# Longer loads in the planner's books, the softmax sums' column left in PSUM, and three slots of the arena given to weights earlier

## The chip, the cores and the metric

One Trainium2 chip; the program runs on one of its cores. The metric is device time in microseconds of one execution, lower is better. Three runs of the kernel before gave 725.32, 720.64 and 724.05 us (median 724.05).

## The reference, cut to what matters

Three stages follow each other, all in float32: rotary attention over B = 4 batches of H = 8 heads (S = 576 tokens, D = 64), a soft mixture of 8 experts with 4 slots each, and a two-layer MLP.

```python
q_rot, k_rot = rotate(q), rotate(k)                      # (4, 8, 576, 64)
scores = q_rot @ k_rot.T / sqrt(64)
attn = exp(scores - max); attn = attn / (attn.sum(-1) + 1e-09)
x = (attn @ v)                                           # 2304 tokens x 512
logits = x @ phi                                         # 512 x 32 slots
slot_input = softmax(logits, over tokens).T @ x          # 8 experts x 4 slots x 512
slot_out[e] = relu(slot_input[e] @ w1[e]) @ w2[e]        # 512 -> 1024 -> 512
x = softmax(logits, over slots) @ slot_out
out = square(relu(x @ w_in)) @ w_out                     # 512 -> 2048 -> 512
```

## The kernel before, in words

**Attention.** Two heads make a *pair* (`NP` = 16 pairs), one head in each half of the 128 partitions. For a pair the kernel:

- loads k, q and their half-swapped copies into one of two buffers `raws[p % 2]` (four slices of 128 x 576; `load`, L296, three DMAs `SEGS` of 64 partitions each, 1152 KB together);
- applies the rotation with six tensor-tensor operations, three for each of k and q (`rope_pair`, L313, recorded at L309, `arena<-arena` in the trace), on VectorE or GpSimd, whichever the planner picks;
- splits each rotated tensor into a rounded half on ScalarE (`parts_pair`, L337, tile `tE`, three buffers `his`) and a remainder on VectorE or GpSimd (L309 again, `tL<-arena,tE`). When both remainders exist, `raws[p % 2]` is free and the load of pair p + 2 can be issued;
- finds each query's maximum: ten *max units* (`max_unit`, TensorE L375, VectorE reduce L382 into `mcol`), then `max_rows`: a reduce L393, a transpose on TensorE L398, a negation L403 into `mrow` and two small DMAs L408 into `mrows[p % 2]`;
- computes the scores in ten *score units* (`st_unit`, TensorE L427 and L431, which adds `mrow`; exponential on ScalarE L440; on GpSimd, L448, the units' sum for the denominator);
- multiplies by V (`pv_unit`, L461) into two fixed PSUM banks, one a head;
- divides (`norm`, L465): the sums of the exponentials by a matmul with ones (L477) into a slot of a PSUM ring, a 32 x 32 block transpose of it on VectorE into `recT` in SBUF (L481), addition of 1e-9 and reciprocal of its column (L486, L487, tile `r`), the transpose back (L491), and the product with the V bank into `xT` (L496). Only then is the V bank free for the next pair;
- adds the pair's share of the logits (`logits`, L515 to L550), and after each fourth pair the slots' share of the batch (`slots_in`).

Scores, maxima, sums and logits share a ring of three PSUM slots (`ring_op`, `take` and `give`).

**Weights.** The experts' w1 and w2 and the MLP's w_in and w_out (48 MB with their 64-bit forms) pass through slots of 1 MB (`LOADS`, `free`, L784): ten slots `w0` to `w9` of their own, filled during attention, and slots that lie on memory the attention has used: `A0` to `A3` on `arena` (the first x, the rope table, V's buffer 0, `raws`), `E0`, `E1` on `tE`, `P0` on `tL`, `P1`, `P2` on `pb` (the sums' accumulators, `xT`, `recT`, V's buffer 1), `O0`, `O1` on `tO`. `gen` lists whose users such a slot waits for.

**Order.** No engine's order is written by hand. All operations go into `Plan.op` with a duration per engine, a due time (in score units) and what they read and write; `Plan.emit` (L105) then plays the program through with these durations and lets each engine take next, among what can start first, the operation with the earliest due time. The order found is fixed when the kernel is built: on the chip each engine's instructions run strictly in it, and each waits for its semaphores. A DMA's length enters as its size: it is taken to finish at 360 KB per us behind the DMA before it (L159). Where the player sees TensorE idle, and a bank is spare (before the first `pv_unit`, between attention and the experts, and after the experts), it puts in dummy matmuls (`fill`, L1410, at L1412), one per `FILL` us of a gap over `GAP` us.

Of the kernel before, what the change touches and what calls it, by code (L numbers as in the profile page):

```python
# [15 lines left out]
ALU = mybir.AluOpType  # L16
# [9 lines left out]
    lod=5.12, b0=1, nwarm=12, sprope=0.8, mxpe=0.0, mxdve=0.1, stpe=0.0,  # L26
    norm=4.2, rope=-22.0, parts=-19.0, v=-7.0, lag=2.5, mr0=0.0, lgt=5.5, slots=6.0,
)
# [10 lines left out]
class Plan:  # L39
# [3 lines left out]
    SPARE = {"DVE": 1.0}  # L43
    FILL = 0.45
    GAP = 0.8
    SWITCH = 0.1
# [122 lines left out]
def kernel(  # L169
# [52 lines left out]

    X0, TAB = 5 * DM, 2 * S + 5 * 2 * D
    RAW = X0 + TAB
# [16 lines left out]
    xT, recT = view(pb, XT, [128, S]), view(pb, XT + S, [128, HQ])  # L241
    vraws = [view(*a, [128, 5, 2, D]) for a in ((arena, X0 + 2 * S), (pb, XT + S + HQ))]
    r9 = pool.tile([128, HQ // 32, 1], F32, name="r9")
# [51 lines left out]
    def load(p, g, ts_, on="SP"):  # L295

        i = p % 2
        for s, (rows, to, of) in enumerate(SEGS):
            q = on if s else "SP"
            dma(  # L300
                lambda rows=rows, to=to, of=of, q=q: QUEUE[q].dma_start(
                    out=raws[i][rows, ts_, to], in_=qk[p][rows, ts_, of]
                ),
                g + 0.01 * s, 590 * len(range(4)[ts_]) / 4 * (to.stop - to.start) / S, (),
                [("raw", i, t, s) for t in range(4)[ts_]], on=q,
            )
# [6 lines left out]
    def rope_pair(p, g):  # L313

        i = p % 2
        on = {0: {"DVE": 0.8}, 1: {"POOL": 1.45}}.get(p, EITHER)
        first = [("hi", 0, 1)] if p == 1 else []
        for t in range(2):
            a, b = raws[i][:, t, :], raws[i][:, t + 2, :]
            ka, kb = ([("raw", i, n, s) for s in range(3)] for n in (t, t + 2))  # L320
            for d, o, x, y, how, reads, writes in (
                (0, a, a, rope_sb[:, 0, :], ALU.mult, [("rope", 0, s) for s in range(3)], ka),
                (1, b, b, rope_sb[:, 1, :], ALU.mult, [("rope", 1, s) for s in range(3)], kb),
                (2, a, a, b, ALU.add, kb, ka),
            ):
                op(
                    on, lambda e, o=o, x=x, y=y, how=how: tt(e, o, x, y, how), g + 3 * t + d, reads + first, writes,
                    spare={"DVE": T["sprope"]},
                )

    def parts_pair(p, g):

        i = p % 2
        for t in range(2):
            a, hi, lo = raws[i][:, t, :], his[p % NHI][:, t, 0:S], los[p % NLO][t][:, 0:S]
            ka, kh, kl = [("raw", i, t, s) for s in range(3)], ("hi", p % NHI, t), ("lo", p % NLO, t)
            op({"ACT": 0.69}, lambda e, a=a, hi=hi: nc.scalar.activation(out=hi, in_=a, func=AF.Copy), g + 3 * t, ka, [kh])  # L337
            op(
                EITHER if p else {"POOL": 1.45}, lambda e, a=a, hi=hi, lo=lo: tt(e, lo, a, f(hi), ALU.subtract), g + 3 * t + 3,
                ka + [kh], [kl], spare={"DVE": T["sprope"]},  # L340
            )
# [123 lines left out]
    def norm(p, h, g):  # L465
# [3 lines left out]
        acc, (rest, rk) = accs[n], p_slot(p, h, 4)  # L469
        col = recT.rearrange("p (b c) -> p b c", c=32)[:, :, 0:1]  # L470
        tok = {}

        def sums(e):
# [5 lines left out]
        op({"PE": 1.1}, sums, g, [("acc", n), rk], [("sm", n)], take="ring", tok=tok, mode="c")  # L479
        ring_op(  # L480
            {"DVE": 0.47}, lambda e: nc.vector.transpose(out=recT, in_=on_ring(tok)[:, 0, 0:HQ]), g, [("sm", n)], ["recT"],  # L481
            give="ring", tok=tok,
        )

        def inverse(e):
            nc.vector.tensor_scalar(out=r9, in0=col, scalar1=1e-9, scalar2=None, op0=ALU.add)  # L486
            nc.vector.reciprocal(out=r9, in_=r9)  # L487

        op({"DVE": 0.37}, inverse, g, ["recT"], ["r9"])
        op(  # L490
# [174 lines left out]
    for slot, kind, e, k in (  # L665
# [18 lines left out]
        **{f"w{i}": [] for i in range(NRING)},  # L684
        "A0": KX0, "A1": KX0 + KTAB + KVR[:1], "A2": KVR[:1] + KRAW[0], "A3": KRAW[0] + KRAW[1], "AX": KRAW[1],
        "E0": KHI[0] + KHI[1], "E1": KHI[1] + KHI[2] + KMR[0], "EX": KMR[0] + KMR[1],
        **{f"O{j}": [("P", 4 * j + i) for i in range(4)] for j in range(2)},
        "P0": KLO,
        "P1": KACC + [("xT", 0), ("xT", 1), "recT"],
        "P2": [("xT", 0), ("xT", 1), "recT", ("vr", 1)],  # L690
        "PX": KLO,
# [124 lines left out]
    for p in range(NP):  # L816
        g0 = NU * p
        gm = g0 - NU - MLEAD
        if p >= 2:
            at(g0 - 39.8, load, p, g0 - 36, slice(0, 4))  # L820
        at(g0 - 28 if p != 1 else -19.8, rope_pair, p, g0 + (T["rope"] if p else -40))
        at(g0 - 19.9 if p != 1 else -9.9, parts_pair, p, g0 + (T["parts"] if p else -38))
# [16 lines left out]
    at(GEND - 30.2, free, "A0", GEND - 30, 2)  # L839
    at(GEND - 7.2, free, "A3", GEND - 7, 2)  # L840
    at(GEND - 6.2, free, "A1", GEND - 6, 2)
    at(GEND + LAG + 0.2, free, "A2", GEND + LAG, 2)
    at(GEND + 0.1, free, "E0", GEND - 3, 2)
# [657 lines left out]
```

## Time and profile before

| what | us |
|---|---|
| median of three runs | 724.05 |
| the profiled execution | 718.12 |
| its span in the profile | 716.3 |
| TensorE busy | 624.6 (87%) |
| VectorE busy | 430.8 (60%) |
| GpSimd busy | 316.1 (44%) |
| ScalarE busy | 269.1 (38%) |
| DMA queue of SP, share of 16 engines | 36.4% |

The profiled execution is one of the program's executions; its own time is its span and 1.8 us around it. The page cuts the span into 40 slices of 17.9 us and gives, per slice, the tenths in which each engine was busy, the clock granted to TensorE and what the DMA engines moved. [...] Three parts of the span differ: attention to about 394 us, the experts to about 450 us, the MLP to the end, of which the last 171 us run from matmul to matmul.

### The profile page before, as it was taken

Reading aid. Unit: us, or ns where it says so; the run is one execution under the profiler, and the core shown is the slowest. Engines: PE = TensorE matmul, PEld = TensorE weight load, DVE = VectorE, ACT = ScalarE, POOL = GpSimd, SP = SyncE. Lnnn points to the kernel's source line nnn. Section 1 sums busy time; section 2 is a strip of 40 time slices with the busy share of each in tenths; the row PEclk is TensorE's granted clock in tenths of the full one; section 3 lists DMA queues with packets and bytes.
Section 4 is the critical chain, followed back from the end, with each engine's and each line's share of the span. In section 5 each row is a group of like instructions: output and inputs, shape, how many; then the busy total and the mean of one; then the engine's idle time right before and its main releaser. Section 6 shows DMA issues by size and latency. Waiting matters only on the chain. (4 is left out here: it accounts for less than half of the span.)

```text
span 716.3 us, 11185 instructions
## 1 busy us (share of the span) xinstructions
PE 624.6 (87%) x4387; PEld 412.3 (58%) x4387; DVE 430.8 (60%) x691; ACT 269.1 (38%) x473; POOL 316.1 (44%) x206
## 2 busy tenths in 40 slices
PE   2688987898889898989998888878799999999997
PEld 2454544554545454555665332546477888888885
DVE  3768766587657776677543541999973344444441
ACT  1123332423334233434333131655554533353332
POOL 2768966577668576793444000265466100000000
PEclk9669999989999899999999999888989999999999
DMA  7375435534563234301103999990000200020002
GB/s 168 72 171 144 118 88 144 144 81 123 144 143 87 60 85 86 86 20 65 73 20 113 393 386 389 397 400 36 1 0 2 89 0 1 0 89 1 0 1 88
DMA packets 36468, 80.75 MB, mean 113 GB/s; under 512 B 7648, under 2 KB 8064, under 8 KB 35456
## 3 DMA queue, kind: packets, MB, share of 16 engines
q1 hardware_dynamic: 35552, 79.16, 36.4%
q10 hardware_dynamic: 864, 0.89, 0.6%
q8 instruction: 34, 0.56, 0.3%
q14 instruction: 18, 0.15, 0.1%
HBM read 75.24 MB, written 4.72 MB: 112 GB/s over the span
## 5 line engine op out<-in xcount | busy, mean ns | idle before, releaser
L440 ACT ACTIVATE tO<-bank 128x576 f32<-128x576 f32 (+1 forms) x160 | 100.9, 648 | 187.5 <-PE bank L431 162.0
L1350 PE MATMUL bank<-w,tE 128*128 128x512 f32 x648 | 165.3, 406 | 0.7 <-DVE tE L1328 0.7
L1350 PEld LDWEIGHTS bank<-w,tE 128*128 128x128 f32 x648 | 124.5, 194 | 28.9 <-DVE tE L1328 1.4
L382 DVE TENSOR_REDUCE mcol<-bank 128x2 f32<-128x576 f32 x160 | 115.5, 746 | 31.7 <-PE bank L375 31.6
L309 POOL TENSOR_TENSOR arena<-arena 128x576 f32<-128x576 f32 x45 | 75.6, 1697 | 58.9 <-DMA arena<-in_qk_dram 55.1
L448 POOL TENSOR_TENSOR pb<-pb,tO 128x576 f32<-128x576 f32 x64 | 92.3, 1442 | 17.7 <-ACT tO L440 15.2
L309 DVE TENSOR_TENSOR arena<-arena 128x576 f32<-128x576 f32 x51 | 65.6, 1294 | 43.5 <-DMA arena<-in_qk_dram 32.2
L375 PE MATMUL bank<-tE 64*128 64x288 f32 x320 | 61.1, 390 | 14.2 <-DVE mrow L403 7.5
L375 PEld LDWEIGHTS bank<-tE 64*128 64x128 f32 x320 | 30.8, 194 | 61.9 <-issue 24.8
L448 POOL TENSOR_TENSOR pb<-tO 128x576 f32<-128x576 f32 x32 | 50.3, 1571 | 35.5 <-ACT tO L440 35.5
L461 PE MATMUL bank<-tO,arena 128*64 128x288 f32 x320 | 58.8, 464 | 8.0 <-DVE pb L496 8.0
L427 PE MATMUL bank<-tE 64*128 64x288 f32 x320 | 56.9, 352 | 8.9 <-DVE mcol L382 7.5
L461 PE MATMUL bank<-tO,pb 128*64 128x288 f32 x320 | 54.2, 431 | 9.8 <-DVE pb L496 9.8
L1350 PE MATMUL bank<-w,tO 128*128 128x512 f32 x216 | 54.6, 403 | 0.0
L427 PEld LDWEIGHTS bank<-tE 64*128 64x128 f32 x320 | 31.2, 192 | 31.2 <-DVE mcol L382 15.5
L427 PE MATMUL bank<-tL,tE 64*128 64x288 f32 x320 | 48.7, 301 | 0.0
L427 PE MATMUL bank<-tE,tL 64*128 64x288 f32 x320 | 48.6, 300 | 0.0
L431 PE MATMUL bank<-tE,pick 64*128 64x288 f32 x320 | 48.6, 300 | 0.0
L1350 PEld LDWEIGHTS bank<-w,tO 128*128 128x128 f32 x216 | 41.0, 192 | 9.9 <-issue 1.2
L309 POOL TENSOR_TENSOR tL<-arena,tE 128x576 fp32r<-128x576 f32 x26 | 37.5, 1455 | 20.0 <-ACT tE L337 19.4
L1258 POOL TENSOR_TENSOR w<-arena,w 128x1024 fp32r<-128x1024 f32 (+1 forms) x9 | 21.9, 2435 | 54.5 <-ACT w L1253 54.5
L1294 ACT ACTIVATE arena<-bank 128x384 f32<-128x384 f32 x48 | 21.8, 489 | 52.5 <-PE bank L1283 52.5
(249 smaller groups left out, 906.8 us busy)
## 6 DMA issues: line engine op xcount, KB each, us to landing
arena<-in_qk_dram SPq DMA_DIRECT2D x15, 576.0 KB
arena<-in_qk_dram SPq DMA_DIRECT2D x15, 512.0 KB
out_dram<-arena SPq DMA_DIRECT2D x18, 256.0 KB
arena<-in_w_dram SPq DMA_DIRECT2D x8, 512.0 KB
tE<-in_w_dram SPq DMA_DIRECT2D x8, 512.0 KB
arena<-in_v_dram SPq DMA_DIRECT2D x8, 320.0 KB
pb<-in_v_dram SPq DMA_DIRECT2D x8, 320.0 KB
w__421<-in_w_dram SPq DMA_DIRECT2D x4, 512.0 KB
```

The costliest lines, as they stand in the source:

```text
L309: ENG[e].tensor_tensor(out=o, in0=x, in1=y, op=how)
L375: nc.tensor.matmul(on_ring(tok)[:, j, 0:HQ], lhsT=hi[rows, 1, UNIT[u]], rhs=hi[rows, 0, HALF[h]], start=True, stop=True)
L382: lambda e: nc.vector.tensor_reduce(out=mcol[:, h, :, u], in_=on_ring(tok)[:, :, 0:HQ], op=ALU.max, axis=AX.X),
L427: nc.tensor.matmul(st[:, j, 0:HQ], lhsT=k[x][rows, UNIT[u]], rhs=q[y][rows, HALF[h]], start=(i == 0), stop=False)
L431: nc.tensor.matmul(st[:, j, 0:HQ], lhsT=pick[rows, :], rhs=mrow[rows, HALF[h]], start=False, stop=True)
L440: lambda e: nc.scalar.activation(out=pr[0:m], in_=on_ring(tok)[0:m, :, 0:HQ], func=AF.Exp, scale=0.125),
L448: lambda e: nc.gpsimd.tensor_tensor(out=acc, in0=one, in1=pr, op=ALU.add),
L461: nc.tensor.matmul(o_t[rows, 0:HQ], lhsT=vr[:, u, j, :], rhs=pr[:, j, :], start=(u == 0), stop=(u == 4))
L1258: lambda e, hs=hs: ENG[e].tensor_tensor(out=wo_of()[:, hs, 1, :], in0=wf_of()[:, hs], in1=f(wo_of())[:, hs, 0, :], op=ALU.subtract),
L1294: lambda e, i=i, h=h: nc.scalar.activation(out=rg_of()[:, 0, h], in_=BANKS[i][:, 0:384], func=AF.Relu),
L1350: nc.tensor.matmul(BANKS[PO[c]], lhsT=gt[:, x, 128 * c : 128 * c + 128], rhs=wo[:, fc % 2, y, :], start=(fc == 0 and i == 0), stop=(fc == ...
```

## The change

The change does seven things.

1. **Loads.** A load of k and q counts 1100 KB for its first segment instead of 590 (and the others in proportion). The transfer itself is the same.
2. **Due times.** The parts of a pair are due one unit earlier (`parts` -20 instead of -19), and within `parts_pair` the steps lie closer together; pair 0's remainders are named as waiting for both rounded halves.
3. **Pair 2.** Its rotation is named as waiting for pair 0's `mrow`, and is recorded later.
4. **The sums' column.** The transpose of the sums writes into the second half of the same ring slot in PSUM, and the addition of 1e-9 reads its column there. The ring slot is given back by that step and no longer by the transpose. `recT` is written only by the transpose back.
5. **V.** Both of V's buffers lie on `pb`; the one on `arena` goes, and `raws` moves down by 640 columns.
6. **Slots.** `A1`, `A2` and `A3` wait for other users (no V among them), and their loads are recorded 20 to 18 units before the end of attention, behind the score units of pair 14, instead of near or after its end. `P1` and `P2` now wait for V.
7. **Fillers.** `FILL` goes from 0.45 to 0.28 us and `GAP` from 0.8 to 0.5 us.

```diff
-    norm=4.2, rope=-22.0, parts=-19.0, v=-7.0, lag=2.5, mr0=0.0, lgt=5.5, slots=6.0,
+    norm=4.2, rope=-22.0, parts=-20.0, v=-7.0, lag=2.5, mr0=0.0, lgt=5.5, slots=6.0,
...
-    FILL = 0.45
-    GAP = 0.8
+    FILL = 0.28
+    GAP = 0.5
...
-    X0, TAB = 5 * DM, 2 * S + 5 * 2 * D
+    X0, TAB = 5 * DM, 2 * S
...
-    vraws = [view(*a, [128, 5, 2, D]) for a in ((arena, X0 + 2 * S), (pb, XT + S + HQ))]
+    vraws = [view(*a, [128, 5, 2, D]) for a in ((pb, XT + S + HQ), (pb, XT + S + HQ + 10 * D))]
...
-                g + 0.01 * s, 590 * len(range(4)[ts_]) / 4 * (to.stop - to.start) / S, (),
+                g + 0.01 * s, 1100 * len(range(4)[ts_]) / 4 * (to.stop - to.start) / S, (),
...
-        first = [("hi", 0, 1)] if p == 1 else []
+        first = {1: [("hi", 0, 1)], 2: [("mrow", 0, 0), ("mrow", 0, 1)]}.get(p, [])
...
-            op({"ACT": 0.69}, lambda e, a=a, hi=hi: nc.scalar.activation(out=hi, in_=a, func=AF.Copy), g + 3 * t, ka, [kh])
+            op({"ACT": 0.69}, lambda e, a=a, hi=hi: nc.scalar.activation(out=hi, in_=a, func=AF.Copy), g + 2 * t, ka, [kh])
             op(
-                EITHER if p else {"POOL": 1.45}, lambda e, a=a, hi=hi, lo=lo: tt(e, lo, a, f(hi), ALU.subtract), g + 3 * t + 3,
-                ka + [kh], [kl], spare={"DVE": T["sprope"]},
+                EITHER if p else {"POOL": 1.45}, lambda e, a=a, hi=hi, lo=lo: tt(e, lo, a, f(hi), ALU.subtract), g + 2 * t + 1,
+                ka + [kh] + ([("hi", 0, 1)] if p == 0 else []), [kl], spare={"DVE": T["sprope"]},
             )
...
-        ring_op(
-            {"DVE": 0.47}, lambda e: nc.vector.transpose(out=recT, in_=on_ring(tok)[:, 0, 0:HQ]), g, [("sm", n)], ["recT"],
-            give="ring", tok=tok,
+        op(
+            {"DVE": 0.47}, lambda e: nc.vector.transpose(out=on_ring(tok)[:, 1, 0:HQ], in_=on_ring(tok)[:, 0, 0:HQ]),
+            g, [], [("sm", n)],
         )
 
         def inverse(e):
+            col = on_ring(tok)[:, 1, 0:HQ].rearrange("p (b c) -> p b c", c=32)[:, :, 0:1]
             nc.vector.tensor_scalar(out=r9, in0=col, scalar1=1e-9, scalar2=None, op0=ALU.add)
             nc.vector.reciprocal(out=r9, in_=r9)
 
-        op({"DVE": 0.37}, inverse, g, ["recT"], ["r9"])
+        ring_op({"DVE": 0.39}, inverse, g, [("sm", n)], ["r9"], give="ring", tok=tok)
...
-        "A0": KX0, "A1": KX0 + KTAB + KVR[:1], "A2": KVR[:1] + KRAW[0], "A3": KRAW[0] + KRAW[1], "AX": KRAW[1],
+        "A0": KX0, "A1": KX0 + KTAB + KRAW[0], "A2": KRAW[0] + KRAW[1], "A3": KRAW[1], "AX": KRAW[1],
...
-        "P1": KACC + [("xT", 0), ("xT", 1), "recT"],
-        "P2": [("xT", 0), ("xT", 1), "recT", ("vr", 1)],
+        "P1": KACC + [("xT", 0), ("xT", 1), "recT"] + KVR,
+        "P2": KVR + ["recT"],
...
-        at(g0 - 28 if p != 1 else -19.8, rope_pair, p, g0 + (T["rope"] if p else -40))
+        at(g0 - 28 if p != 1 and p != 2 else -19.8 if p == 1 else -3.9, rope_pair, p, g0 + (T["rope"] if p else -40))
...
-    at(GEND - 7.2, free, "A3", GEND - 7, 2)
-    at(GEND - 6.2, free, "A1", GEND - 6, 2)
-    at(GEND + LAG + 0.2, free, "A2", GEND + LAG, 2)
+    for n, k in enumerate(("A1", "A2", "A3")):
+        at(GEND - 19.8 + n, free, k, GEND - 20 + n, 2)
```

Two lists of `gen` (`E0`, `E1`) are also written out in full. What the change does to the built order stands in four pieces. From L480 on its line numbers are one lower. In them `L309 ... arena<-arena` is a step of the rotation, `L309 ... tL<-arena,tE` a remainder, L382 the reduce of a max unit.

VectorE at the opening, from the last reduce of pair 0 (`mcol_106`) on; before:

```order
L382 TENSOR_REDUCE mcol_106<-bank_84 128x2
L309 TENSOR_TENSOR arena<-arena 128x576
L393 TENSOR_REDUCE m_108<-mcol_106 128x10
L309 TENSOR_TENSOR arena<-arena 128x576
L403 TENSOR_SCALAR mrow_107<-bank_85 10x128
L309 TENSOR_TENSOR arena<-arena 128x576 x2
L309 TENSOR_TENSOR tL<-arena,tE 128x576
L309 TENSOR_TENSOR arena<-arena 128x576
L382 TENSOR_REDUCE mcol_109<-bank_86 128x2
```

VectorE at the same place with the change:

```order
L382 TENSOR_REDUCE mcol_106<-bank_84 128x2
L309 TENSOR_TENSOR tL<-arena,tE 128x576
L393 TENSOR_REDUCE m_108<-mcol_106 128x10
L403 TENSOR_SCALAR mrow_107<-bank_85 10x128
L382 TENSOR_REDUCE mcol_109<-bank_86 128x2
L382 TENSOR_REDUCE mcol_109<-bank_84 128x2
L382 TENSOR_REDUCE mcol_109<-bank_85 128x2
L309 TENSOR_TENSOR arena<-arena 128x576
```

The five rotation steps that stood among pair 0's `mrow` and ahead of pair 1's reduces (`mcol_109`) come later; a remainder of pair 1 has moved up.

TensorE at the opening, between the warm-up matmuls (L1422, now L1421) and the first max units; before:

```order
L1422 MATMUL bank_87<-arena 128x128 x12
L375 MATMUL bank_84<-tE 128x288 x2
L375 MATMUL bank_85<-tE 128x288 x2
L375 MATMUL bank_86<-tE 128x288 x2
```

TensorE at the same place with the change:

```order
L1421 MATMUL bank_87<-arena 128x128 x12
L1411 MATMUL bank_87<-es 128x128 x13
L375 MATMUL bank_84<-tE 128x288 x2
L375 MATMUL bank_85<-tE 128x288 x2
L375 MATMUL bank_86<-tE 128x288 x2
L1411 MATMUL bank_87<-es 128x128
```

Fourteen fillers have come in there. Further on, around pair 0's transpose (L398), the runs of fillers go from 5, 6 and 2 to 10, 4 and 1; after the attention 14 stand where 4 did, and in the experts' second half and the start of the MLP 20 where 7 did.

VectorE at pair 7's rotation and pair 4's `mrow`, about 113 to 124 us in the trace of before:

```order
L491 STREAM_TRANSPOSE pb<-r_83 128x288
L309 TENSOR_TENSOR arena<-arena 128x576
L496 TENSOR_TENSOR pb<-bank_87,pb 128x288
L382 TENSOR_REDUCE mcol_106<-bank_86 128x2
L382 TENSOR_REDUCE mcol_106<-bank_84 128x2
L309 TENSOR_TENSOR arena<-arena 128x576
L527 TENSOR_TENSOR lg_70<-lg_70,bank_86 128x192
L393 TENSOR_REDUCE m_108<-mcol_106 128x10
L309 TENSOR_TENSOR arena<-arena 128x576
L403 TENSOR_SCALAR mrow_107<-bank_86 10x128
```

VectorE at the same place with the change:

```order
L491 STREAM_TRANSPOSE pb<-r_83 128x288
L496 TENSOR_TENSOR pb<-bank_87,pb 128x288
L382 TENSOR_REDUCE mcol_106<-bank_86 128x2
L382 TENSOR_REDUCE mcol_106<-bank_85 128x2
L527 TENSOR_TENSOR lg_70<-lg_70,bank_84 128x192
L393 TENSOR_REDUCE m_108<-mcol_106 128x10
L309 TENSOR_TENSOR arena<-arena 128x576 x2
L403 TENSOR_SCALAR mrow_107<-bank_85 10x128
L309 TENSOR_TENSOR arena<-arena 128x576
```

Pair 7's first rotation step has moved behind the product L496, two reduces, the logits' sum and L393; two steps stand ahead of L403 and one behind it. Counted in max units, the first step moves so by two for pairs 6, 7, 10, 11, 14 and 15; it stays at its count for pairs 8, 12 and 13 and comes two earlier for pair 9. Of the remainders 12 are on VectorE instead of 6, and 20 on GpSimd instead of 26.

SP's queue at pair 8's load (`w__1076` and `w__1095` are the same slot, `w4`); before:

```order
L346 DMA pb<-in_v_dram 128x640
L301 DMA arena<-in_qk_dram 64x2304
L784 DMA w__1076<-in_w_dram 128x1024 x2
L301 DMA arena<-in_qk_dram 64x4x512
L301 DMA arena<-in_qk_dram 64x4x64
```

SP's queue at the same place with the change:

```order
L346 DMA pb<-in_v_dram 128x640
L301 DMA arena<-in_qk_dram 64x2304
L301 DMA arena<-in_qk_dram 64x4x512
L301 DMA arena<-in_qk_dram 64x4x64
L784 DMA w__1095<-in_w_dram 128x1024 x2
```

The megabyte of weights has moved from between the three segments to behind them. The same holds for pairs 9 and 12; for pairs 10, 11 and 14 the load of V now stands ahead of all three segments, where before one or two were ahead of it. Near the start, V of pair 2 now stands ahead of slot `w0`'s weights, and these directly ahead of pair 5's load. At the end of attention `A1` stands ahead of the last load of V, and `A2` and `A3` between that and the last pair's `mrow`.

## Rows read from the trace of the kernel before

**Rows 1.** The page: its head, and the granted clock of the 40 slices.

```profile
span 716.3 us, 11185 instructions
...
PEclk9669999989999899999999999888989999999999
```

**Rows 2.** Windows: length, busy us (and instructions) of PE, PEld, DVE, ACT, POOL; clock, DMA, GB/s.

```profile
60.00:80.00 20.00, 17.50 (x170) 10.68 (x170) 16.83 (x28) 6.60 (x12) 17.56 (x11) 1.00 0.42 109
...
120.00:140.00 20.00, 18.86 (x186) 11.29 (x178) 15.02 (x28) 8.01 (x14) 13.75 (x10) 1.00 0.44 117
...
260.00:280.00 20.00, 17.98 (x176) 11.05 (x176) 15.25 (x27) 8.16 (x14) 16.42 (x11) 1.00 0.32 68
...
60.00:320.00 260.00, 226.37 (x2042) 135.15 (x2044) 184.71 (x315) 94.29 (x167) 187.47 (x123) 0.95 0.42 105
...
320.00:387.00 67.00, 65.48 (x639) 39.88 (x639) 35.65 (x78) 26.71 (x51) 32.04 (x23) 1.00 0.13 43
```

**Rows 3.** Waits of PE and DVE from 90 to 310 us: total us, times, longest.

```profile
PE bank L461 <- DVE pb L496: 17.1, 9, 2.9
PE bank L375 <- DVE mrow L403: 7.0, 6, 3.0
PE bank L427 <- DVE mcol L382: 4.3, 5, 2.9
...
DVE arena L309 <- DMA arena<-in_qk_dram: 26.7, 10, 3.6
```

**Rows 4.** Timeline, pairs 7 and 8: start us, length, what, [idle before <- releaser].

```profile
117.37 0.76 DVE L309 TENSOR_TENSOR arena<-arena 128x576 f32<-128x576 f32 x1 [3.44 <-DMA arena<-in_qk_dram]
118.04 0.45 DVE L496 TENSOR_TENSOR pb<-bank,pb 128x288 f32<-128x288 f32 x1
118.41 1.42 DVE L382 TENSOR_REDUCE mcol<-bank 128x2 f32<-128x576 f32 x2
119.74 1.63 DVE L309 TENSOR_TENSOR arena<-arena 128x576 f32<-128x576 f32 x1
...
118.55 1.19 PE L461 MATMUL bank<-tO,pb 128*64 128x288 f32 x8 [2.77 <-DVE pb L496]
...
143.13 0.76 DVE L309 TENSOR_TENSOR arena<-arena 128x576 f32<-128x576 f32 x1 [2.94 <-DMA arena<-in_qk_dram]
```

**Rows 5.** Timeline of SP's queue: the first DMA of pair 7's and of pair 8's load.

```profile
107.96 1.84 SPq L301 DMA_DIRECT2D arena<-in_qk_dram  x3
...
130.58 0.55 SPq L301 DMA_DIRECT2D arena<-in_qk_dram  x1
131.18 1.10 SPq L784 DMA_DIRECT2D w__1076<-in_w_dram  x2
```

**Rows 6.** Timeline of the opening, TensorE and VectorE.

```profile
14.19 4.69 PE L1422 MATMUL bank<-arena 128*128 128x128 f32 x24 [14.19 <-DVE arena L309]
...
24.50 2.34 PE L1412 MATMUL bank<-es 128*128 128x128 f32 x10
...
37.97 0.61 PE L427 MATMUL bank<-tE 64*128 64x288 f32 x2
...
28.78 1.68 DVE L309 TENSOR_TENSOR arena<-arena 128x576 f32<-128x576 f32 x1 [2.68 <-DMA arena<-in_qk_dram]
...
32.26 0.27 DVE L403 TENSOR_SCALAR mrow<-bank 10x128 fp32r<-10x128 f32 x1
```

**Rows 7.** The column's addition: all 32 by form; a column read from PSUM, from the timeline.

```profile
L486 DVE TENSOR_SCALAR r<-pb 128x9 f32<-128x9 f32 x32 | 13.1, 411 | 0.2
...
402.32 0.15 DVE L1041 TENSOR_SCALAR den<-bank 128x1 f32<-128x1 f32 x1
```

**Rows 8.** SP's loads into the arena's slots; TensorE's waits for DMA in the experts.

```profile
336.24 1.80 SPq L784 DMA_DIRECT2D arena<-in_w_dram  x4
...
388.12 2.17 SPq L784 DMA_DIRECT2D arena<-in_w_dram  x4
...
PEld bank L1120 <- DMA tE<-in_w_dram: 0.8, 2, 0.5
```

More of the change, by code (lines that the diff above doesn't have):

```diff
@@ L469, in norm @@
         acc, (rest, rk) = accs[n], p_slot(p, h, 4)
-        col = recT.rearrange("p (b c) -> p b c", c=32)[:, :, 0:1]
         tok = {}
@@ L684 @@
         **{f"w{i}": [] for i in range(NRING)},
-        "A0": KX0, "A1": KX0 + KTAB + KVR[:1], "A2": KVR[:1] + KRAW[0], "A3": KRAW[0] + KRAW[1], "AX": KRAW[1],
-        "E0": KHI[0] + KHI[1], "E1": KHI[1] + KHI[2] + KMR[0], "EX": KMR[0] + KMR[1],
+        "A0": KX0, "A1": KX0 + KTAB + KRAW[0], "A2": KRAW[0] + KRAW[1], "A3": KRAW[1], "AX": KRAW[1],
+        "E0": KHI[0] + KHI[1], "E1": KHI[0] + KHI[1] + KHI[2] + KMR[0] + KMR[1], "EX": KMR[0] + KMR[1],
         **{f"O{j}": [("P", 4 * j + i) for i in range(4)] for j in range(2)},
         "P0": KLO,
-        "P1": KACC + [("xT", 0), ("xT", 1), "recT"],
-        "P2": [("xT", 0), ("xT", 1), "recT", ("vr", 1)],
+        "P1": KACC + [("xT", 0), ("xT", 1), "recT"] + KVR,
+        "P2": KVR + ["recT"],
         "PX": KLO,
```

## The prediction, made before the changed kernel ran

> **What bounds the kernel now.** I read the page first, then windows of 20 us, then who waited for whom, then the timeline around the longest waits. The span is 716.3 us [rows 1]. The windows split the attention in two. From 320 to 387 us nothing is rotated any more (all q and k have been loaded), and TensorE is busy 65.48 of 67 us at full clock: 639 matmuls, 9.54 a us. From 60 to 320 us it does 2042 in 260 us, 7.85 a us, at a mean clock of 0.95 [rows 2]. At the later pace these 2042 would take 214.1 us; so some 46 us are lost there, and they are what this change can reach.
>
> The waits say where. From 90 to 310 us TensorE waits 17.1 us for the product L496, 7.0 for `mrow` and 4.3 for reduces, 28.4 together, all on VectorE; and VectorE itself waits ten times, 26.7 us, for a load of q and k [rows 3]. The timeline joins the two: VectorE stands 3.44 us before pair 7's first rotation step, the short product L496 stands behind it in the queue, and TensorE, which needs the V bank, gets on at 118.55 after 2.77 us of nothing [rows 4]. The rotation was not urgent; the player put it there because it had the load finished earlier than the chip has. A load takes 117.37 - 107.96 = 9.4 us from its first issue to its user's start, and 143.13 - 130.58 = 12.5 where a megabyte of weights is issued between its segments [rows 4, 5]. The lost clock is the second part: 0.05 of 260 us is 13 us of full-speed time, and 28.4 + 13 = 41 of the 46 us are accounted for. The last 171 us of the MLP I leave alone: no edit touches them.
>
> **The change part by part.**
>
> *Loads counted longer (1), with the due times of the parts (2).* The bytes stay; only the order moves. For pair 7 the first step moves behind L496 (0.45 us), two reduces (1.42) and two small steps, so by at least 1.9 us [rows 4], and what now stands behind a late load is `mrow` and no longer L496. The same holds for six pairs of ten: 6 x 1.9 = 11.2 us of VectorE's waits. For pairs 8, 9 and 12 the weights leave the load, worth up to 12.5 - 9.4 = 3.1 us each, more than pair 8's wait of 2.94 [rows 4]; I count 2.5 each, 7.5. Together 18.7 of 26.7, that is 70%. If TensorE's waits shrink alike, 0.70 x 28.4 = 20 us go; if half of the lost clock comes back, another 6.5. That makes 26.5. A second way, by windows: the three that hold no wait or only a short one for a load, 60 to 80, 120 to 140 and 260 to 280, do 170, 186 and 176 matmuls [rows 2], a mean of 177.3 in 20 us; at that pace 2042 take 230.3 us, 29.7 less than 260. At the slowest of the three, 170, they take 240.2, 19.8 less. I take **-25**. The ends are -46 (the pace after 320 us) and +20 (the slower rival below). Against the full 29.7 speaks that VectorE (184.7) and GpSimd (187.5 us) would then be busy over 80% of the stretch themselves [rows 2], and that V is now ahead of three loads and a megabyte of weights ahead of pair 5's.
>
> What is late next where the stalls go: TensorE's own work, with the reduces and GpSimd's sums close behind.
>
> *Opening (2, 3, 7).* Before, the ten reduces of pair 0 end at 28.78 - 2.68 = 26.10 us, then VectorE waits for pair 2's load with pair 0's `mrow` behind it; `mrow` comes at 32.26 and the first score unit at 37.97, since the reduces of pair 1 stand behind more rotation [rows 6]. With the change nothing of pair 2 stands ahead of `mrow`. Against it stand the fillers. Before the first max unit 13 come in. In the warm-up one cost 4.69 / 12 = 0.39 us (two of the 24 records each), after 24.50 one cost 2.34 / 5 = 0.47, at a granted clock of 0.50 (the low slices of [rows 1]); at the upper level it should be half of 0.47, an estimate. So 13 delay the max units by 3.0 to 5.1 us. The reduces then end at about 29 to 31, and the transpose of the maxima stands behind ten more fillers (2.3 to 4.7 us, beside the last reduces in part): `mrow` comes at about 30.5 to 33. After it only four fillers, three max units and their reduces remain, so the first score unit comes at 34 to 39 instead of 37.97. I take **-2.5**, with ends -6 (no filler costs anything) and +3.
>
> *The sums' column (4).* L486 took 0.411 us on average over its 32 times; a column read from PSUM took 0.15 (L1041), and the negation of `mrow`, 128 columns from PSUM, 0.27 [rows 6, 7]. So 32 x (0.411 - 0.27 to 0.15) = 4.5 to 8.4 us of VectorE go, on the way to L496. The trace has no transpose from PSUM into PSUM; nearest are the product that reads 288 columns (0.45) and the reduce that reads 576 (0.71) [rows 4]: between nothing and 0.26 more each, 0 to 8.3 us. The ring slot is held longer by about a reduce and the column's read, 0.9 us, 32 times; the player knows that, and the waits for reduces (4.3 us, rows 3) say how scarce the ring is. Only a part of all this is on TensorE's way: I take **-1.5**, ends -8.4 and +8.
>
> [...]
>
> *V's place and the slots (5, 6).* Of the three slots one goes early already: at 336.24 four half-megabyte pieces leave, `A0` and `A3`; only `A1` and `A2` wait until 388.12 [rows 8]. So two megabytes move into a stretch in which the DMA engines are idle (share 0.13, rows 2). But the experts hardly wait for weights: TensorE's weight loads wait 0.8 us for the last of them [rows 8], and VectorE's order of the conversions around the experts' end is the same in both. That is -0.8 at most. Their cover is that the slots are read late; if it were gone, 2.1 MB at 43 / 0.13 = 331 GB/s (the row of 320 to 387 us, scaled to a full share, an estimate) would be 6.3 us. The thirteen more fillers in the experts' end and the MLP's start, and ten after attention, cost 0.39 us each if no gap held them, 9 us; they are put only where the player has found a gap. I take **+0.5** for both, near the cover's side since the one wait seen is 0.8 us, with ends -0.8 and +9. `A2` and `A3` ahead of the last `mrow` in SP's queue wait for the last pair's remainders and score unit 142, 8 units before that pair's first score unit; nothing.
>
> **Sum.** -25 - 2.5 - 1.5 + 0.5 = -28.5 on the profiled execution's 718.1, which gives 689.6. The median of the runs, 724.05, stands 5.9 above that execution; the forecast for the median of the changed kernel is **695.5 us**.
>
> **The rivals.**
>
> *Half of it.* The waits are VectorE's and GpSimd's as much as the loads': the same rotation step takes 0.76 us and, two steps later, 1.63 [rows 4], and with the pace both engines' operations meet more often. For it: the 80% above, and six remainders more on VectorE. Against it: the stall-free windows have the same contention. Then half the waits go, -12.5 instead of -25: 708.
>
> [...]
>
> *All of it.* The late pace holds from 60 us on, with no stall and no lost clock: -46 instead of -25, 674.5. Against it: after 320 us VectorE had 35.7 us of work in 67, before it 184.7 in 260 [rows 2].
>
> *No gain.* The order does what it says, but the loads land later by as much: V ahead of three, weights ahead of one, each gated by slots that come free with TensorE's own pace; within 7 us of 724.
>
> *Slower.* The loads land behind the player's new figure too, and then a late load stands ahead of `mrow`, which gates every score unit of the next pair, where it stood ahead of L496. That is what pair 8 had, and the slice that holds it (143 to 161 us) shows a clock of 0.8, two tenths of 17.9 us or some 3 us on top of the wait [rows 1, 4]. For the six pairs moved there that is 3.3 us more each than now: +20, 744. It decides if VectorE reaches the step over 3 us before the load has landed; it now reaches it 1.9 us later than when it waited 2.67 on average.
>
> **How the numbers follow.** Forecast 0.50 (with its own range of 686 to 704), half 0.22, all 0.10, none 0.12, slower 0.06. No change and 1% are told apart at 7.2 us, about what a measurement of this kernel can do: under 716.8 is faster. The forecast, all, and nearly all of the half (0.21) lie there: 0.81 with what is left for the tail of the first; slower than 731.3 only the last, 0.06; the rest, 0.13, within. Leaving a tenth on either side, the range is 683 to 717 us.
>
> **What would show it.** Right: VectorE's waits for loads from 90 to 310 us under 8 us, TensorE's for L496 under 8, the clock at 0.98 or more from 60 to 320, the 2042 matmuls done in some 235 us; the first score unit at 35 to 36; L486's successor at 0.15 to 0.28; the arena's slots issued before the end of attention and the experts as long as before. Wrong: the same waits under another name (`mrow` instead of L496), a low clock in every pair, or an opening that ends later than before.

## The result, and the profile after

The median went from 723.32 to **699.01 us**; the ratio is 0.966, with a 95% interval of 0.962 to 0.970. Forecast were 695.5, within 683 to 717. One run of the changed kernel (766.77 us, clock 0.75) and one of a kernel below (the number taken back: 845.72 us, 0.65) ran slow, at a lower granted clock, and enter no ratio. The profiled execution took 699.11 us where that of before took 718.12: 19.0 less. The marks on the way tell where they went. `mrow` of pair 0 comes 1.2 us later (33.46 for 32.26), `mrow` of pair 1 3.7 us earlier (51.94 for 55.62), `mrow` of the last pair 21.2 us earlier, and from there to the end the changed kernel takes 352.3 us for 350.2. So the stretch from the first `mrow` to the last gives 22.4 us, 4.9 of them before the second `mrow`, and 2.2 us are given back after it. The last `mrow`, before and after:

```profile
367.96 0.28 DVE L403 TENSOR_SCALAR mrow<-bank 10x128 fp32r<-10x128 f32 x1 [0.73 <-PE bank L398]
```

```profile
346.78 0.28 DVE L403 TENSOR_SCALAR mrow<-bank 10x128 fp32r<-10x128 f32 x1 [0.99 <-PE bank L398]
```

The head of the page after, and its clock by slices; what it answers to is [rows 1]:

```profile
span 697.3 us, 11351 instructions
...
PEclk9899989999999899999999999989999999999999
```

The windows of the changed kernel, columns as in [rows 2] (the second stretch is the one after its last rotation):

```profile
60.00:320.00 260.00, 231.06 (x2186) 140.21 (x2182) 202.78 (x344) 100.77 (x183) 187.77 (x120) 0.96 0.42 107
...
300.00:367.00 67.00, 66.10 (x673) 41.75 (x675) 36.09 (x83) 28.33 (x54) 36.37 (x28) 1.00 0.23 81
```

In the same 260 us TensorE does 2186 matmuls and not 2042: 8.41 a us for 7.85. This window reaches further past the last rotation step than before; up to that step it is 8.29 a us (1956 from 60 to 296 us) for 7.83 (1972 from 60 to 312). The clock rose by 0.01 only.

The waits from 90 to 310 us (engine, tile, line <- whom; total us, times, longest), after:

```profile
POOL arena L309 <- DMA arena<-in_qk_dram: 30.8, 9, 4.6
...
PE bank L427 <- DVE mcol L382: 14.0, 10, 4.5
...
PE bank L375 <- DVE mrow L403: 7.9, 8, 1.5
...
DVE arena L309 <- DMA arena<-in_qk_dram: 6.7, 6, 2.0
...
PE bank L461 <- DVE pb L496: 1.5, 2, 0.7
```

Against [rows 3]: VectorE waits 6.7 us for loads and not 26.7, and TensorE 1.5 for L496 and not 17.1. But TensorE's waits for `mcol` grew from 4.3 to 14.0, and GpSimd still waits for loads. Its row before was:

```profile
POOL arena L309 <- DMA arena<-in_qk_dram: 50.9, 10, 9.0
```

The opening after, TensorE and VectorE, against [rows 6]:

```profile
19.62 3.24 PE L1411 MATMUL bank<-es 128*128 128x128 f32 x26
22.79 0.66 PE L375 MATMUL bank<-tE 64*128 64x288 f32 x6
...
28.58 4.63 PE L1411 MATMUL bank<-es 128*128 128x128 f32 x20
...
36.33 0.40 PE L427 MATMUL bank<-tE 64*128 64x288 f32 x2 [0.27 <-DVE mcol L382]
...
33.46 0.28 DVE L403 TENSOR_SCALAR mrow<-bank 10x128 fp32r<-10x128 f32 x1 [1.78 <-PE bank L398]
```

Thirteen fillers (two records each) now stand ahead of the first max unit, and ten more ahead of the transpose that `mrow` waits for. The first score unit comes at 36.33 for 37.97.

The sums' transpose and the column's addition, all 32 by form, against [rows 7]:

```profile
L480 DVE STREAM_TRANSPOSE bank<-bank 128x288 f32<-128x288 f32 x32 | 15.9, 496 | 31.8 <-PE bank L476 31.7
...
L486 DVE TENSOR_SCALAR r<-bank 128x9 f32<-128x9 f32 x32 | 4.9, 154 | 0.1
```

The addition fell from 411 to 154 ns, 8.2 us over 32; the transpose, into PSUM now, rose from 482 to 496.

SP's issues into the arena's slots, against [rows 8]:

```profile
317.85 0.81 SPq L784 DMA_DIRECT2D arena<-in_w_dram  x2
331.23 0.81 SPq L784 DMA_DIRECT2D arena<-in_w_dram  x2
336.94 1.86 SPq L784 DMA_DIRECT2D arena<-in_w_dram  x4
```

All eight pieces leave before the attention ends. Still the experts are no shorter: from the first product with an expert's weights to the end of the last group of L1119 (before L1120) pass 47.5 us (380.21 to 427.72), before 46.1 (402.07 to 448.20).

### The profile page after: what moved, and what is told of

It reads as the page before. It is cut to its first block, busy times and chain, and to the rows that moved or that the text cites. A ratio compares the mean times of both kernels' runs of the same rounds, so it can differ in the third digit from the quotient of the medians.

```text
span 697.3 us, 11351 instructions
## 1 busy us (share of the span) xinstructions
PE 615.0 (88%) x4465; PEld 412.7 (59%) x4465; DVE 437.7 (63%) x697; ACT 268.8 (39%) x473; POOL 310.9 (45%) x200
## 5 line engine op out<-in xcount | busy, mean ns | idle before, releaser
L1349 PE MATMUL bank<-w,tE 128*128 128x512 f32 x648 | 163.2, 402 | 2.1 <-DVE tE L1327 1.9
L382 DVE TENSOR_REDUCE mcol<-bank 128x2 f32<-128x576 f32 x160 | 115.3, 746 | 33.0 <-PE bank L375 32.9
L461 PE MATMUL bank<-tO,pb 128*64 128x288 f32 x640 | 107.5, 434 | 2.6 <-DVE pb L496 2.4
L448 POOL TENSOR_TENSOR pb<-pb,tO 128x576 f32<-128x576 f32 x64 | 94.4, 1475 | 12.5 <-ACT tO L440 8.8
L309 POOL TENSOR_TENSOR arena<-arena 128x576 f32<-128x576 f32 x45 | 76.4, 1714 | 34.5 <-DMA arena<-in_qk_dram 30.8
L309 DVE TENSOR_TENSOR arena<-arena 128x576 f32<-128x576 f32 x51 | 69.5, 1379 | 21.6 <-DMA arena<-in_qk_dram 17.8
L427 PE MATMUL bank<-tE 64*128 64x288 f32 x320 | 59.7, 370 | 17.9 <-DVE mcol L382 16.2
L427 PEld LDWEIGHTS bank<-tE 64*128 64x128 f32 x320 | 30.6, 188 | 56.0 <-DVE mcol L382 22.0
L375 PE MATMUL bank<-tE 64*128 64x288 f32 x320 | 49.2, 343 | 12.6 <-DVE mrow L403 7.9
L461 PEld LDWEIGHTS bank<-tO,pb 128*64 128x64 f32 x640 | 35.5, 137 | 31.3 <-issue 16.2
L375 PEld LDWEIGHTS bank<-tE 64*128 64x128 f32 x320 | 28.6, 189 | 34.7 <-issue 12.7
L1304 DVE TENSOR_TENSOR pb<-pb 128x768 f32<-128x768 f32 (+1 forms) x17 | 15.9, 934 | 40.6 <-ACT pb L1293 40.6
```

What stands on the lines that cost most here:

```text
L309: ENG[e].tensor_tensor(out=o, in0=x, in1=y, op=how)
L375: nc.tensor.matmul(on_ring(tok)[:, j, 0:HQ], lhsT=hi[rows, 1, UNIT[u]], rhs=hi[rows, 0, HALF[h]], start=True, stop=True)
L382: lambda e: nc.vector.tensor_reduce(out=mcol[:, h, :, u], in_=on_ring(tok)[:, :, 0:HQ], op=ALU.max, axis=AX.X),
L427: nc.tensor.matmul(st[:, j, 0:HQ], lhsT=k[x][rows, UNIT[u]], rhs=q[y][rows, HALF[h]], start=(i == 0), stop=False)
L448: lambda e: nc.gpsimd.tensor_tensor(out=acc, in0=one, in1=pr, op=ALU.add),
L461: nc.tensor.matmul(o_t[rows, 0:HQ], lhsT=vr[:, u, j, :], rhs=pr[:, j, :], start=(u == 0), stop=(u == 4))
```

## The experiments

My theory was that the loads stand too early in VectorE's queue, and that this one number carries the gain. Its rivals were that the other edits carry it, and that the waits would only move to VectorE's and GpSimd's own work. Ratios are to the kernel before, timed on the same chip.

**Loads made short, order untouched.** In the kernel before, each DMA of a load moves a quarter of its columns from pair 2 on:

```diff
+            n = (to.stop - to.start) // (4 if p >= 2 else 1)
+            put, of = slice(to.start, to.start + n), slice(of.start, of.start + n)
...
-                    out=raws[i][rows, ts_, to], in_=qk[p][rows, ts_, of]
+                    out=raws[i][rows, ts_, put], in_=qk[p][rows, ts_, of]
```

> The kernel before with its order untouched, but from pair 2 on each DMA of a load of q and k moves a quarter of its columns; the other columns keep what an earlier pair left, so three quarters of the data are left out from pair 2 on. My theory: late loads in front of VectorE's queue cost the 28.4 us of TensorE's waits and some lost clock; with nothing late, VectorE waits under 3 us for loads from 90 to 310 us, TensorE under 5 for L496, and the time falls by 20 to 30 us, to 694 to 704. Rival (the waits are VectorE's and GpSimd's own work, and the order's details made the gain): the waits for loads go but others take their place, and the time falls by less than 8 us, 716 or more.

Measured: 690.02 us, ratio 0.957 (0.952 to 0.962). The window and the waits (two lines of source have been added, so L463 and L498 are L461 and L496):

```profile
60.00:320.00 260.00, 244.35 (x2310) 146.67 (x2310) 202.61 (x353) 105.34 (x189) 188.43 (x130) 0.99 0.24 75
```

```profile
PE bank L463 <- DVE pb L498: 6.1, 8, 1.4
...
DVE arena L311 <- DMA arena<-in_qk_dram: 0.3, 1, 0.3
```

The order that looked bad is a good one once its loads are in time: 8.88 matmuls a us, the clock at 0.99. The 31 us are more than the 20 to 30 expected, while TensorE still waits 6.1 us for L496, not under 5. So late loads cost the kernel before up to 31 us. (The short loads also take traffic off the queue, 75 GB/s in this window for 105; what that gives V and the weights is not told apart.)

**The one number alone.** `590` to `1100` in the kernel before, nothing else.

> The kernel before with one number changed, 1100 for 590 in the size of a load. My theory: this one number carries most of the gain, 15 to 25 us, so 699 to 709, with VectorE's waits for loads from 90 to 310 us under 10 and TensorE's for L496 under 8. Rival: the gain needs the due times and the rest as well, and this alone gives under 6 us, 718 or more.

Measured: 696.58 us, ratio 0.965 (0.960 to 0.971).

```profile
60.00:320.00 260.00, 244.31 (x2230) 142.35 (x2228) 208.66 (x355) 102.82 (x185) 186.15 (x117) 0.98 0.43 111
```

```profile
PE bank L427 <- DVE mcol L382: 9.1, 12, 2.5
...
DVE arena L309 <- DMA arena<-in_qk_dram: 3.8, 5, 1.6
```

One number gives what the whole change gives (0.965 beside 0.966): 24.3 us, of 15 to 25 expected. TensorE's wait for L496 is gone from the list, and the clock is back to 0.98.

It was the place of the user, and not a shorter load. SP's queue at pair 8's load in this kernel, and the load's first user:

```profile
123.31 0.54 SPq L301 DMA_DIRECT2D arena<-in_qk_dram  x1
...
125.20 1.06 SPq L784 DMA_DIRECT2D w__1082<-in_w_dram  x2
126.30 0.55 SPq L301 DMA_DIRECT2D arena<-in_qk_dram  x1
...
136.37 0.76 DVE L309 TENSOR_TENSOR arena<-arena 128x576 f32<-128x576 f32 x1 [1.58 <-DMA arena<-in_qk_dram]
```

The megabyte of weights still stands between the segments, and from the first issue to the user pass 13.1 us, before 12.5 [rows 4, 5]. But `mrow` now stands ahead of the late step and comes at 133.41; before it stood behind the step, which starts at 143.13 there. VectorE waits 1.58 us and not 2.94.

**The one number taken back.** `1100` to `590` in the changed kernel.

> The changed kernel with 590 back in the size of a load, all else as changed. My theory: the late loads come back with the waits, 718 to 728, VectorE's waits for loads from 90 to 310 us over 20 us. Rival (the due times and the rest would do without it): 706 or less.

Measured: 725.76 us, ratio 1.004 (0.999 to 1.008). The six other edits together give nothing, and the waits are back:

```profile
PE bank L461 <- DVE pb L496: 31.4, 7, 5.6
...
DVE arena L309 <- DMA arena<-in_qk_dram: 28.1, 8, 4.0
```

**The due times and pair 2 alone**, in the kernel before:

> The kernel before with the due times of a pair's parts, the named waits of pair 0's remainders and pair 2's later rotation alone. My theory: without the longer loads these change little, 4 us either way (720 to 728), but the opening's first score unit comes before 37 us. Rival: the due times carry over 10 us of the gain, 713 or less.

Measured: 717.20 us, ratio 0.993 (0.990 to 0.995). The time is 3.6 us below 720.84, just under the 720 to 728 expected. The first score unit comes at 31.44 us and not 37.97; VectorE's waits for loads stay at 23.3 us, and from 60 to 320 us TensorE does 2044 matmuls for 2042. So these edits act in the opening, and are worth some 4 to 5 us by themselves.

```profile
31.44 0.40 PE L427 MATMUL bank<-tE 64*128 64x288 f32 x2 [0.27 <-DVE mcol L382]
```

**The column alone**, in the kernel before (the edits at L481 to L487 of the diff), and **the column taken back**, in the changed kernel:

> The kernel before with the sums' column left in PSUM alone. My theory: the column's addition falls from 411 ns to about 150, the transpose stays near 0.48 us, 8 us of VectorE go, and of that 1 to 3 us of the time: 721 to 723. Rival: the ring slot held longer costs more than the column gives, 728 or more.

> The changed kernel with the sums' column transposed into recT again. Theory A (with the loads counted right the column is a gain, since it was only late loads before L496 that turned it into a loss in the kernel before): 700 to 704, slower than the changed kernel. Theory B (the ring slot held longer costs in any order): 694 or less, with TensorE's waits for mcol from 90 to 310 us well under the changed kernel's 14.0.

Measured: 728.62 us, ratio 1.012 (1.009 to 1.015), with the column alone; 701.70, ratio 0.974 (0.970 to 0.977), with the column taken back, where the changed kernel has 0.966 (0.962 to 0.970). The addition took 151 ns in the first, as expected, and yet that kernel lost 8 us, where 1 to 3 of gain were expected:

```profile
PE bank L461 <- DVE pb L496: 31.7, 8, 5.3
...
DVE arena L309 <- DMA arena<-in_qk_dram: 31.5, 9, 4.5
...
143.59 0.76 DVE L309 TENSOR_TENSOR arena<-arena 128x576 f32<-128x576 f32 x1 [3.60 <-DMA arena<-in_qk_dram]
144.27 0.47 DVE L491 STREAM_TRANSPOSE pb<-r 128x288 f32<-128x288 f32 x1
...
146.14 0.44 DVE L496 TENSOR_TENSOR pb<-bank,pb 128x288 f32<-128x288 f32 x1
```

The player has placed rotation steps one place further up: at eight of eleven late loads from 60 us on the step stands ahead of L491, before at two of ten, so the late load holds back the transpose and L496 too. With the loads counted longer the same edit is no loss. Whether it is a gain is open: the two ratios of the changed kernel, whose intervals touch, say 3 to 5 us, but the loads and the column alone, below, are no faster than the loads alone (0.967 and 0.965). That the ring slot costs it is not borne out by the time.

**The fillers taken back**, in the changed kernel (`FILL = 0.45`, `GAP = 0.8`):

> The changed kernel with FILL and GAP as before (0.45 and 0.8). Theory A (the fillers cost nothing and only hold the clock up): 699 to 704, max units start 4 us earlier, the clock is at its lower level from about 25 to 40 us again. Theory B (they delay the opening by more than the clock gives back): 693 to 697.

Measured: 694.82 us, ratio 0.962 (0.957 to 0.967), in theory B's range; but against 0.966 the intervals overlap. The trace, of an execution of 700.44 us, shows two opposite effects:

```profile
32.86 0.40 PE L427 MATMUL bank<-tE 64*128 64x288 f32 x2 [0.26 <-DVE mcol L382]
```

```profile
PEclk9999989989899899999995999798899999999999
```

The first score unit comes 3.5 us earlier without the extra fillers; but between attention and experts a slice stands at 0.5, and from the last product with V to the first with an expert's weights pass 17.0 us (362.87 to 379.87) for 14.1 with them (366.13 to 380.21). That the fillers make this second difference is not shown: the kernel before, without the extra ones, takes 13.9 there (388.17 to 402.07). In the opening they bought no clock: the window from 30 to 40 us shows 0.97 without them and 0.82 with them (0.50 in the kernel before).

**V's place and the slots taken back**, in the changed kernel:

> The changed kernel with V's buffers, the slots' waits and the place of their loads as before. My theory: the experts and the MLP take as long as with the change, 697 to 701, the same within 2 us. Rival (the earlier weights save the time of two megabytes): 704 or more.

Measured: 694.01 us, ratio 0.962 (0.959 to 0.965); the rival is out, and the early weights save nothing. The time lies below the 697 to 701 expected. In its trace the middle and the end are both shorter: from the first `mrow` to the last 309.7 us (32.38 to 342.10) for 313.3, and from there to the span's end 347.6 for 350.5.

**What is put together from the better parts.** The loads, due times, pair 2 and the column, without fillers and slots; and the loads and the column alone:

> The kernel before with the loads, the due times, pair 2 and the column, without the fillers, V's place and the slots. My theory: fillers and slots each cost the changed kernel 3 to 5 us and are independent, so 686 to 692. Rival (the two runs without one of them were lucky orders): 694 or more.

> The kernel before with the longer loads and the column alone. Theory A (the column is a gain once loads are counted right): 690 to 695, below the 696.6 of the longer loads alone. Theory B (the two pairs of 28 us that all kernels with the column and longer loads show, and the longer loads alone do not, eat it): 697 to 702, with mrow's cadence above 26 us at the sixth and tenth pair.

Measured: 697.86 us, ratio 0.965 (0.959 to 0.970), and 699.07, ratio 0.967 (0.961 to 0.972). The first lies in its rival's range: the two gains of 5 us did not add up, so neither is shown. The second lies in theory B's: the column is no gain on top of the longer loads alone (696.58, 0.965). Both kernels have two long pairs, the sixth and the tenth, of 27 to 29 us from `mrow` to `mrow`, as the changed kernel has; the longer loads alone do not (23.1 and 22.3). With the column and the longer loads alone they are there, so the due times are not needed for them; the changed kernel with the column taken back has them too (27.0 and 27.9), so neither is the column. What makes them is open; what they are made of can be read. The tenth pair of the changed kernel, VectorE, GpSimd and TensorE:

```profile
224.60 1.95 DVE L309 TENSOR_TENSOR arena<-arena 128x576 f32<-128x576 f32 x1 [1.10 <-POOL arena L309]
226.47 1.35 DVE L612 SCALAR_TENSOR_TENSOR ssum<-ssum,al,rsum 128x1 f32<-128x1 f32 x1
227.85 1.32 DVE L613 SCALAR_TENSOR_TENSOR ssum<-rsum,ssum 128x1 f32<-128x1 f32 x1
229.09 1.41 DVE L382 TENSOR_REDUCE mcol<-bank 128x2 f32<-128x576 f32 x2
```

```profile
221.21 3.36 POOL L309 TENSOR_TENSOR arena<-arena 128x576 f32<-128x576 f32 x2 [3.98 <-DMA arena<-in_qk_dram]
224.53 1.40 POOL L448 TENSOR_TENSOR pb<-tO 128x576 f32<-128x576 f32 x1
225.89 1.91 POOL L309 TENSOR_TENSOR arena<-arena 128x576 f32<-128x576 f32 x1
227.77 2.87 POOL L448 TENSOR_TENSOR pb<-pb,tO 128x576 f32<-128x576 f32 x2
```

```profile
229.90 0.61 PE L427 MATMUL bank<-tE 64*128 64x288 f32 x2 [4.46 <-DVE mcol L382]
```

GpSimd waits 3.98 us for the load; VectorE's step waits for GpSimd's; two sums of one column each then take 1.35 and 1.32 us; and only then comes the reduce that TensorE has been waiting for, for 4.46 us. After that idle stretch its matmuls are at a lower clock: 0.50 is granted from 229 to 232 us, and a pair of them takes 0.61 us where such a pair took 0.40 at 222.58, at 1.00.

**Those sums behind the reduces**, on the kernel without fillers and slots:

```diff
-        op({"DVE": 0.33}, sums, g + 0.5, [("rs", 0), ("rs", 1), "al"], ["ssum"])
+        op({"DVE": 0.33}, sums, g + 0.5, [("rs", 0), ("rs", 1), "al", "e"], ["ssum"])
```

> As c_ldpn, but the sums of the slots' weights (three operations on 128x1, L608, L612, L613) wait for the copies of es and so stand behind three reduces instead of ahead of them. My theory (what is left is VectorE's other work, slowed beside GpSimd, ahead of the reduces that score units wait for): the two long pairs fall from 28 us to 24 to 26, TensorE's waits for mcol from 60 to 320 us from about 13 to under 10, the time by 3 to 6 us. Rival (the long pairs come from elsewhere): the same within 2 us.

Measured: 697.37 us, ratio 0.964 (0.958 to 0.969): the same. The two pairs did shrink, to 25.0 and 23.5 us, but pairs beside them grew (the seventh from 19.2 to 21.9, the eleventh from 18.2 to 19.4). TensorE's waits for `mcol` from 60 to 320 us were 11.2, not under 10, and 11.3 without this edit. So these sums explain part of the two long pairs, and no time.

**The changed kernel with short loads**, edited as in the first run:

> The changed kernel, order untouched, with a quarter of each load from pair 2 on as in the earlier run on the kernel before (three quarters of the data are left out). Theory A (what is left is VectorE's and GpSimd's own work): the time stays at 695 to 700, with the two pairs of 28 us. Theory B (the loads still come late, now before GpSimd's rotation, 30.8 us of its waits): 685 to 692, and the long pairs shrink below 24 us.

Measured: 671.04 us, ratio 0.930 (0.924 to 0.935); 28 us below the changed kernel.

```profile
60.00:320.00 260.00, 248.96 (x2462) 153.53 (x2460) 206.37 (x379) 110.48 (x200) 193.62 (x128) 0.99 0.27 83
```

```profile
PE bank L429 <- DVE mcol L384: 4.0, 2, 2.8
```

Theory B holds and was too small. Up to its last rotation step TensorE does 9.34 matmuls a us (1924 from 60 to 266 us), a pace that the kernel before keeps up only after its own (626 from 312 to 379). The two long pairs are 23.0 and 25.9, the second not under 24, and the waits of GpSimd and VectorE for loads are no longer on the list. Here too the traffic that is left out is not told apart from the lateness.

## Why the prediction was right, and where not

- **Middle, -25.** The mechanism is the one named, and the one number alone gives 24 to 25 us: VectorE's waits for loads fell from 26.7 to 6.7 us (forecast under 8) and TensorE's for L496 to 1.5 (under 8). Within the changed kernel the size is somewhat smaller: 22.4 us from the first `mrow` to the last, 17.5 from the second. The forecast marks it by 235 us for 2042 matmuls; at 2186 in 260 us they take 242.9, and the clock is 0.96 where 0.98 was named. The longer loads alone show both nearly as written (238.1 us, 0.98).
- **The working of that term** holds for the longer loads alone and not for the changed kernel. It let TensorE's three waits shrink with VectorE's, from 28.4 to about 8, and half of the lost clock come back. With the one number they are 9.3 us (9.1 for `mcol`, 0.2 for `mrow`, none for L496), at 0.98. With the column added to it they are 19.9 (11.0, 8.0 and 0.9), at 0.95, and in the changed kernel 23.4 (14.0, 7.9 and 1.5), at 0.96: the wait under another name that the prediction set down as a sign of being wrong, in part. That these kernels are as fast even so is luck as far as the working goes. In the changed kernel the matmuls from 60 to 320 us take TensorE 106 ns each instead of 111; why is not shown. Of the 18.7 us that the working adds up for VectorE, 7.5 were for weights that leave three loads; with the one number they still stand within those of pairs 8 and 12, and the waits are gone all the same.
- **Opening, -2.5.** Smaller than forecast at the mark that was named, larger one pair on: the first score unit comes 1.6 us earlier, at 36.33 (inside 34 to 39, past the 35 to 36 named as a sign), `mrow` of pair 0 at 33.46, past the 30.5 to 33, and `mrow` of pair 1 3.7 us earlier. Both halves are there, the 6.5 us that the order gives alone (31.44 for 37.97), and some 3.5 that the fillers take back. The thirteen ahead of the first max unit ran at a granted clock of 1.00 and took 3.24 us, 0.25 each; the ten ahead of the transpose ran at 0.50 and took 4.63, 0.46 each, so the estimate of half held.
- **Column, -1.5.** The operation was priced right (0.154 us against 0.15 to 0.27; the transpose 14 ns dearer, the low end of its bounds). What it is worth depends on the order around it: 8 us lost alone, nothing to be seen on top of the longer loads, perhaps 3 to 5 gained within the changed kernel. The working took the gain for the price of the read; the rows say that it is GpSimd's time that is no longer waited for (last section). The 32 additions from PSUM take 4.9 us in all, those from SBUF took 13.1, and the 14 of the latter with no GpSimd operation beside them took 0.15 to 0.17 us each, about as long as those from PSUM (0.14 to 0.17).
- **Slots and fillers, +0.5.** Right in kind: no gain from either. 2.2 us went after the last `mrow`; which edit they belong to is open: with the slots taken back this stretch is 2.9 us shorter, but with the longer loads alone, and nothing of slots or fillers, it is 350.2 us to the span's end, as long as with the change (350.5; before 348.3).
- **The rivals.** *Slower* did not come: no late load stands ahead of `mrow` for long (7.9 us of waits for 7.0), but the same thing happens one step on, at `mcol`. *All of it* was held unlikely since VectorE has much more work before 320 us than after. That reason has fallen: with short loads the changed order reaches 671.0 us, beside the 674.5 worked out for that rival, and holds the late pace with VectorE busy 170 and GpSimd 165 of the 206 us up to its last rotation step. So the late pace was not kept back by these engines' work but by the loads, by their lateness or by their traffic.
- **Median.** The -28.5 was made against an execution of 718.12 that lay below the three runs then known; between the medians it is -24.3, between the profiled executions -19.0.

What is left can be read from the code and one pair. The player counts a load of k and q as 1100 x (1 + 512/576 + 64/576) / 360 = 6.1 us after 1.4 of issue, before 3.3. On the chip, in the tenth pair above, pair 12's load goes out at 211.67 and GpSimd starts on it at 221.21: 9.5 us. A larger number was not tried; that it would reach the short loads' time is not shown, since short loads also take traffic off the queue (83 GB/s from 60 to 320 us for 107).

## What to carry to other kernels

Where a planner fixes each engine's order, measure a transfer from its issue to the start of its user, with V and weights around it, and give the planner that time: a user placed too early holds back what stands behind it (in the kernel before, VectorE stood 3.44 us ahead of one rotation step, and TensorE waited 2.77 for the L496 behind it [rows 4]). Before mending an order, run it with the suspected transfer made short and nothing else changed; that gives the price, at most, in one run, and once more afterwards it tells how much can be left (here nearly as much again). And a small edit has no price of its own in such a kernel: the column lost 8 us alone and nothing beside the longer loads, by what the player made of it.

## What was not expected of the hardware

Two sums over a 128x1 column took 1.35 and 1.32 us beside GpSimd, in the tenth pair above; in the kernel with the longer loads alone the same two took 0.56 and 0.16:

```profile
219.47 0.56 DVE L612 SCALAR_TENSOR_TENSOR ssum<-ssum,al,rsum 128x1 f32<-128x1 f32 x1 [0.53 <-ACT al L604]
220.07 0.16 DVE L613 SCALAR_TENSOR_TENSOR ssum<-rsum,ssum 128x1 f32<-128x1 f32 x1
```

The first long one ends at 227.82, when GpSimd's step does (225.89 + 1.91 = 227.80), and the second at 229.17, about when the first of GpSimd's two sums does (227.77 + 2.87/2 = 229.2). The 0.56 us in the other kernel end at 220.03, as a sum of GpSimd does (218.60 + 1.41 = 220.01). So by these three ends their length is GpSimd's remaining time and not their own.

The column's addition shows the same, and what its read from PSUM saves. In the kernel before, reading from SBUF, and with the change, reading from PSUM, each beside a sum of GpSimd:

```profile
151.89 1.92 POOL L448 TENSOR_TENSOR pb<-pb,tO 128x576 f32<-128x576 f32 x1
153.04 0.80 DVE L486 TENSOR_SCALAR r<-pb 128x9 f32<-128x9 f32 x1
```

```profile
64.50 3.41 POOL L448 TENSOR_TENSOR pb<-pb,tO 128x576 f32<-128x576 f32 x2
66.12 0.15 DVE L486 TENSOR_SCALAR r<-bank 128x9 f32<-128x9 f32 x1
```

Before, 18 of the 32 additions began while GpSimd was at work on an operation. They took 0.17 to 1.25 us, and 17 of them ended 0.03 to 0.04 us after that operation (here 153.84 after 153.81); the other 14 took 0.15 to 0.17. With the change 24 of the 32 began beside GpSimd, and all 32 took 0.14 to 0.17.
